# Issue order of the first loads, place of one block's statistics, and time of the last loads of x in a fused layernorm, state-space and gated-MLP kernel

## The chip, the cores and the metric

The kernel runs on one core of one Trainium2 chip. The metric is the device time in microseconds (us) of one execution. Three runs of the kernel before the change gave a median of 200.94 us (200.86 to 201.03).

## What is computed

The input x is one sequence of 2048 tokens with 512 features. The reference, cut to what matters:

```python
xn = _layernorm(x, axis=-1)
# A: a diagonal complex state-space model over the tokens
Lam_bar = exp(dt * Lam);  B_bar = ((Lam_bar - 1) / Lam)[:, None] * Bmat
Bu = einsum("bld,pd->blp", xn, B_bar)
h[t] = Lam_bar * h[t-1] + Bu[:, t]
A = 2 * einsum("blp,dp->bld", hseq, Cmat).real + xn * Dskip
# B: a gated MLP with 1792 hidden features
B = (silu(xn @ w1) * (xn @ w3)) @ w2
return x + A + B
```

The output is bfloat16, and so are x and all the weights.

## The kernel before the change, in words

**Tiling.** The 2048 tokens are four blocks (0 to 3) of 512 tokens; a block is four chunks of 128 tokens, one token on each partition. A chunk of x is 128 KB. All of x has its home in one tile, `x_all`, of which `x_blk[b]` is block b. Weights w1 and w3 are loaded by columns; a tile of 128 hidden features is called f here (f = 0 to 13).

**A block's way.** Layernorm: mean and variance of each chunk (`ln_stats`, L219 and L220, VectorE), the reciprocal root, the normalized chunk `xn` (`ln_apply`, L224), and its transpose `xnT` (TensorE and ScalarE in block 0, L243 and L244; a transposing DMA on SP's queue in the other blocks, L247). Then `glu(b)`: for each f four matmuls with w1 and four with w3 into PSUM tiles `gu_ps` (L587), copied out by ScalarE (L596, L597) and multiplied on VectorE (L604, "gate"). In the midst of it `bu(b)` makes the state inputs (L454, copied out into `u` at L456). VectorE turns `u` by tables of cosines and sines (L484, L488, L493), scans it (L505) and turns it back (L513, L519); POOL adds the two halves by accumulating DMAs (L527). Last comes `y_fast` (L1054): seven matrix products for each pair of chunks, with sums of the operands made on VectorE (L1000, L1005, L1096) and by POOL's accumulating DMAs (L1007, L1093).

**The start.** Block 0 can't wait for whole weights. L164 to L170 issue, ahead of everything: each of chunks 0 and 1 of x as two halves, the left half on SP's queue and the right half on ScalarE's; chunk 3 on ScalarE's queue and chunk 2 on SP's; then four weight loads of 256 KB on SP's queue: w1 columns 0 to 255, w3 columns 0 to 255 (for f = 0 and 1), w1 and w3 columns 256 to 511 (f = 2 and 3). TensorE runs warm-up matmuls on a tile of ones (L196), transposes chunk 0 and 1, and does `quarter(cl, fs)` (L619): 128 tokens of one chunk by the first three f. Its order is chunk 0 and then 1 with f = 0, 1; the transpose of the parameter rows (L315); transposes of chunk 2; chunk 0 with f = 2; transposes of chunk 3; chunk 1 with f = 2; then chunks 2 and 3. `bulk_loads` (L172 to L180) issues the rest of w1 and w3, x of block 1 and the state weights on SP's queue, held back by a small ScalarE instruction (L173) that reads the first reciprocal root. SP's queue is in order: a DMA that waits holds back all behind it.

**The filler.** VectorE's work for later stages stands in a queue of tasks, `bg`, each with an estimated cost; `bg.fill` and `bg.flush` take tasks from its head while the program text is built, so that the order on each engine is fixed beforehand. At the head stand (L1169 to L1174): the angles of the second half of the tables (`table_angles(2, 2)`, L376 to L380), the four chunk statistics of block 1 (`ln1a`) and the reciprocal root on POOL (`finish_stats`, L254, L255), the four `ln_apply` with their transposing DMAs (`ln1b`), and then `late_loads` (L182 to L186), which issues on SP's queue w2, the skip row, the four chunks of x of block 2, and x of block 3 in one piece. Behind these come the tasks of `ssm_tasks(0)`, block 0's state pipeline.

**Later readers that the prediction speaks of.** The x of block 2 is first read by ScalarE at L274 (sums for the layernorm of block 2). `res_list` has POOL add x of a block into `xn` by an accumulating DMA (L937). The row sums of the first pair of chunks, `row_sums(0)` (L1000), are written over the x of blocks 0 and 1, so they wait until these accumulating DMAs have read it.

Of the kernel before, what the change touches and what calls it, by code (L numbers as in the profile page):

```python
# [17 lines left out]
P = 128  # L18
# [45 lines left out]
def kernel(  # L64
# [17 lines left out]
    nc = tc.nc  # L82
    _, S, D = A_x.shape
# [25 lines left out]
    xv = A_x[0].rearrange("(c p) d -> p c d", p=P)  # L109
# [40 lines left out]
    x_all = xpool.tile([P, NBLK, CPB, D], BF16, name="x_blk")  # L150
    x_blk = [x_all[:, i] for i in range(NBLK)]
# [3 lines left out]
    def load_w(f0, f1, eng1=nc.sync, eng3=nc.sync):  # L155
        eng1.dma_start(out=w1_sb[:, :, f0:f1], in_=w1v[:, :, f0:f1])
        eng3.dma_start(out=w3_sb[:, :, f0:f1], in_=w3v[:, :, f0:f1])

    def load_x(b, parts=1):
        n = CPB // parts  # L160
        for i in range(0, CPB, n):
            nc.sync.dma_start(out=x_blk[b][:, i:i + n, :], in_=xv[:, b * CPB + i:b * CPB + i + n, :])

    for c in range(2):  # L164
        for eng, dsl in ((nc.sync, slice(0, D // 2)), (nc.scalar, slice(D // 2, D))):
            eng.dma_start(out=x_blk[0][:, c, dsl], in_=xv[:, c, dsl])  # L166
    nc.scalar.dma_start(out=x_blk[0][:, 3, :], in_=xv[:, 3, :])
    nc.sync.dma_start(out=x_blk[0][:, 2, :], in_=xv[:, 2, :])
    load_w(0, 2 * P)
    load_w(2 * P, 4 * P)  # L170

    def bulk_loads():  # L172
# [9 lines left out]
    def late_loads():  # L182
        nc.sync.dma_start(out=w2_sb, in_=B_w2.rearrange("(t p) d -> p t d", p=P))
        nc.sync.dma_start(out=dskip_row, in_=A_Dskip.partition_broadcast(P))
        load_x(2, 4)
        load_x(3)  # L186

# [23 lines left out]
    bg = Filler(LEAD)  # L211
# [37 lines left out]
    def ln_tasks_vector(b):  # L249
        csl = slice(b * CPB, (b + 1) * CPB)  # L250

        def finish_stats():
            vpe = lnp.tile([P, CPB], FP32, name="vpe")
            nc.gpsimd.tensor_scalar(out=vpe, in0=mv_all[:, csl, 1], scalar1=LN_EPS, scalar2=None, op0=ALU.add)  # L254
            nc.gpsimd.tensor_tensor(out=rstd_all[:, csl], in0=vpe, in1=mhalf, op=ALU.pow)  # L255

        def apply(cl):
            if cl == 0:
                ln_alloc(b)
            ln_apply(b, cl)  # L260
            ln_transpose(b, cl)

        first = [(0.85, lambda cl=cl: ln_stats(b, cl)) for cl in range(CPB)] + [(0.0, finish_stats)]
        second = [(0.4, lambda cl=cl: apply(cl)) for cl in range(CPB)]
        return first, second
# [74 lines left out]
    def sin_step(until=None):  # L340
        while sins and (until is None or until not in sins_done):
            key, fn = sins.popleft()
            fn()
            sins_done.add(key)
            if until is None:
                break
# [23 lines left out]
    def table_angles(pt, n=1):  # L370
        if pt + n > 3:
            sin_step((pt + n - 4, 0))
        slots = scratch[:, 0:2 * NPT * 2 * TBLK].bitcast(FP32).rearrange("p (h i t) -> p h i t", h=2, t=TBLK)
        ang, rnd = slots[:, 0, pt:pt + n, :], slots[:, 1, pt:pt + n, :]
        for i in range(n):
            nc.vector.tensor_scalar(out=ang[:, i, :], in0=iota_f, scalar1=turn[:, pt + i:pt + i + 1], scalar2=None,  # L376
                                    op0=ALU.mult)
        nc.vector.tensor_scalar(out=rnd, in0=ang, scalar1=MAGIC, scalar2=None, op0=ALU.add)
        nc.vector.scalar_tensor_tensor(out=ang, in0=rnd, scalar=MAGIC, in1=ang, op0=ALU.subtract, op1=ALU.subtract)
        nc.vector.tensor_scalar(out=rnd.bitcast(DT.int32), in0=ang.bitcast(DT.int32), scalar1=0x7FFFFFFF, scalar2=None,  # L380
                                op0=ALU.bitwise_and)
        for k in range(pt, pt + n):
            for i, (src, bias, scale) in enumerate(((rnd, halfpi, -TWO_PI), (ang, 0.0, -TWO_PI))):
                sins.append(((k, i), lambda k=k, i=i, src=src[:, k - pt, :], bias=bias, scale=scale: nc.scalar.activation(
                    out=tabe[:, k, i, :], in_=src, func=ACT.Sin, bias=bias, scale=scale)))
# [76 lines left out]
    def ssm_tasks(b, posts_last=False, between=(), middle=(), late=()):  # L462
# [76 lines left out]
        def add(*fns):  # L539
            for fn in fns:  # L540
                bg.add(0.0 if fn in transfers else 1.2 if fn in scans0 or fn in scans1 else 1.16, fn,
                       ("scan", b) if fn in scans0 else ("post", b) if fn in post0 else ("ssm", b))

        if b == 0:
            add(*pre0, *scans0, *post0, *pre1, *scans1, *post1)
            return
        add(*pre0)
        for t in middle:
# [32 lines left out]
    def glu(b):  # L581
# [76 lines left out]
        for f in range(f0, NFT):  # L658
            if f == AHEAD[b]:
                if b == 0:  # L660
                    ssm_tasks(0)
                if b == 2:
                    sin_step(("squares", 3, CPB - 1))
                    bg.flush(("bu", 0))
                    steps.extend(bu_fast(b, 0))
                    second = lambda: bu_fast(b, 1)
                else:
                    bu(b)
# [497 lines left out]

    ln_alloc(0)
    ln1a, ln1b = ln_tasks_vector(1)
    bg.add(3.6, lambda: table_angles(2, 2))  # L1169
    for t in ln1a:  # L1170
        bg.add(*t)
    for t in ln1b:
        bg.add(*t, ("ln", 1))
    bg.add(0.0, late_loads, ("ln", 1))  # L1174
    bg.add(0.2, params_w)
    gate = glu(0)
# [33 lines left out]
    def keep_ends(b):  # L1210
# [3 lines left out]
        nc.vector.tensor_copy(out=ends, in_=act(b)[:, CPB - 1].rearrange("p (h k) t -> p h k t", h=2)[:, :, NFH:NK, P - 1])  # L1214

    ssm_tasks(1, between=[(0.2, lambda: keep_ends(0))])
    gate = glu(1)
    gate()
# [6 lines left out]
    for cl, o in held:  # L1225
        nc.sync.dma_start(out=ov[:, cl, :], in_=o)
    bg.add(*difference(1))
    ssm_tasks(2, between=res_list(3), late=[(0.2, lambda: keep_ends(1)), *row_sums(2, *pairs[2]), *column_sums(3)])
    bg.first(bu_sums(2))
    gate = glu(2)  # L1230
# [52 lines left out]
```

## Time and profile before

| what | value |
|---|---|
| median of three runs | 200.94 us |
| span of the profiled execution (first to last instruction) | 199.5 us |
| around the span (median less span) | 1.4 us |
| busy: PE, DVE, ACT, POOL | 195.6, 181.8, 135.0, 51.5 us |
| share of PE in the chain that ended last | 95% |
| TensorE clock granted in the mean | 0.999 |

The page gives one time for the profiled execution, its span; the runs' times are longer by what lies ahead of the first and behind the last instruction. PE is TensorE, PEld its weight loads, DVE is VectorE, ACT ScalarE, POOL GpSimd, SPq the queue that SyncE issues DMAs on. A timeline row gives the start, the duration, the engine and line, the operation with output and inputs, the number of instructions merged into the row, and in brackets the engine's idle time ahead of it with what ended it. A row of windows gives the busy time of each engine in a stretch with the number of instructions, the granted clock, the busy share of the 16 DMA engines (over 1 where packets overlap) and the rate.

### The profile page before, as it was taken

How to read it: one execution, taken by the hardware profiler on the slowest of the kernel's cores; microseconds unless marked ns; L12 is line 12 of the kernel's file. 1: busy time of each engine (PE TensorE's matmuls, PEld its weight loads, DVE VectorE, ACT ScalarE, POOL GpSimd, SP SyncE). 2: the span in 40 equal slices, each digit the busy share in tenths (PEclk: the TensorE clock that was granted, in tenths of full speed). 3: DMA queues.
4: the chain of work that ended last, by engine and by line, in shares of the span. 5: the costliest groups of instructions: out<-in, count | busy, mean ns of one | idle time of the engine just before them, and what ended most of it. 6: DMA issues, size and time to landing. Idle time of an engine off the chain costs nothing.

```text
span 199.5 us, 3700 instructions
## 1 busy us (share of the span) xinstructions
PE 195.6 (98%) x1401; PEld 130.7 (65%) x1401; DVE 181.8 (91%) x254; ACT 135.0 (68%) x281; POOL 51.5 (26%) x75
## 2 busy tenths in 40 slices
PE   8999999999999999999999999999999999999994
PEld 2774444444444488866555468888566678888893
DVE  3689699999999999989999997999999999999972
ACT  4699897699999996968998684362588783111220
POOL 7180289700411134041202305040021303310000
PEclk9999999999999999999999999999999999999999
DMA  4999996991497054730997455838137732941111
GB/s 138 326 277 200 302 186 124 343 273 23 69 181 141 0 105 82 135 105 0 156 148 119 89 92 98 172 83 132 53 59 129 149 56 52 174 92 36 53 44 40
DMA packets 32258, 25.12 MB, mean 126 GB/s; under 512 B 16240, under 2 KB 29936, under 8 KB 32240
## 3 DMA queue, kind: packets, MB, share of 16 engines
q0 software_dynamic: 6128, 11.38, 33.5%
q1 hardware_dynamic: 25536, 13.21, 26.8%
q10 hardware_dynamic: 576, 0.30, 0.5%
q8 instruction: 11, 0.18, 0.4%
q14 instruction: 7, 0.06, 0.1%
HBM read 7.74 MB, written 2.10 MB: 49 GB/s over the span
## 4 chain that ended last, share of the span: by engine, by line
PE 95%; DMA 2%; SPq 1%; issue 0%; DVE 0%
PE gu_ps L587 34%; PE gu_ps L1054 17%; PE y_ps L1054 10%; PE gu_ps L848 7%; PE bu_ps L1054 7%; PE bu_ps L454 3%; PE y_ps L454 3%; PE y_ps L869 3%; PE y_ps L780 3%; DMA w_sb<-in_B_w_dram 2%; PE gu_ps L619 2%; PE gu_ps L780 2%; PE bu_ps L869 1%; PE bu_ps L780 1%; PE bu_ps L619 1%; SPq L166 0%
## 5 line engine op out<-in xcount | busy, mean ns | idle before, releaser
L587 PE MATMUL gu_ps<-xnT,w_sb 128*128 128x512 bf16 x312 | 69.6, 379 | 0.0
L587 PEld LDWEIGHTS <-w_sb 128*128 128x128 bf16 x312 | 30.5, 98 | 34.2
L1054 PEld LDWEIGHTS <-act 128*128 128x128 f16 x462 | 43.5, 98 | 5.4
L596 ACT ACTIVATE g<-gu_ps 128x512 bf16<-128x512 f32 x41 | 24.8, 606 | 6.0 <-PE gu_ps L587 3.6
L597 ACT ACTIVATE u<-gu_ps 128x512 bf16<-128x512 f32 x41 | 24.8, 606 | 4.5 <-PE gu_ps L587 3.7
L505 DVE TENSOR_TENSOR_SCAN u<-rho,ends,u 128x512 bf16<-128x512 f32 x16 | 20.0, 1270 | 0.0
L527 POOL DMA_DIRECT2D act<-p x7 | 9.2, 1320 | 34.0 <-DVE act L519 22.1
L1054 PE MATMUL gu_ps<-w_sb,act 128*128 128x256 bf16 (+3 forms) x126 | 16.0, 267 | 0.0
L848 PE MATMUL gu_ps<-xnT,w_sb 128*128 128x512 bf16 x64 | 15.9, 379 | 0.0
L604 DVE TENSOR_TENSOR act<-g,u 128x1024 f16<-128x1024 bf16 x21 | 14.2, 679 | 0.4 <-ACT u L597 0.4
L860 ACT ACTIVATE g<-gu_ps 128x512 bf16<-128x512 f32 x14 | 8.4, 599 | 5.4 <-PE gu_ps L848 5.0
L454 PEld LDWEIGHTS <-bt 128*128 128x128 bf16 x64 | 6.3, 98 | 7.5
L1077 ACT ACTIVATE x_blk<-gu_ps 128x256 f32<-128x256 f32 (+1 forms) x9 | 3.3, 368 | 10.6 <-PE gu_ps L1054 10.6
L1054 PE MATMUL bu_ps<-w_sb,act 128*128 128x256 bf16 (+3 forms) x84 | 10.4, 264 | 0.0
L1054 PE MATMUL gu_ps<-ct,act 128*128 128x256 f16 (+1 forms) x72 | 10.4, 267 | 0.0
L848 PEld LDWEIGHTS <-w_sb 128*128 128x128 bf16 x64 | 6.3, 98 | 4.8
L505 DVE TENSOR_TENSOR_SCAN u<-rho,u 128x512 bf16<-128x512 f32 x8 | 9.2, 1206 | 0.0
L1054 PEld LDWEIGHTS <-x_blk 128*128 128x128 f16 x88 | 8.6, 98 | 1.0
L1054 PEld LDWEIGHTS <-tw 128*128 128x128 f16 x88 | 8.6, 98 | 1.0
L513 DVE TENSOR_TENSOR p<-u,tabe 128x2048 f16<-128x2048 bf16 (+1 forms) x8 | 8.7, 1085 | 0.1
L519 DVE TENSOR_TENSOR act<-u,tabe 128x2048 f16<-128x2048 bf16 (+1 forms) x8 | 8.7, 1083 | 0.0
L488 DVE TENSOR_TENSOR u<-u,tabe 128x2048 bf16<-128x2048 bf16 x7 | 8.5, 1219 | 0.1
(203 smaller groups left out, 392.5 us busy)
## 6 DMA issues: line engine op xcount, KB each, us to landing
act<-p POOLq DMA_DIRECT2D x6, 512.0 KB, 6.1
xn<-x_blk POOLq DMA_DIRECT2D x4, 512.0 KB, 5.5
out_dram<-xn SPq DMA_DIRECT2D x15, 128.0 KB, 1.7
w_sb<-in_B_w_dram SPq DMA_DIRECT2D x1, 1792.0 KB, 8.2
act<-act POOLq DMA_DIRECT2D x5, 352.0 KB, 4.6
w_sb<-in_B_w_dram SPq DMA_DIRECT2D x2, 768.0 KB, 6.4
u<-p POOLq DMA_DIRECT2D x3, 512.0 KB, 5.1
w_sb<-in_B_w_dram SPq DMA_DIRECT2D x4, 256.0 KB, 4.9
```

The lines of the kernel that those rows point to most:

```text
L454: nc.tensor.matmul(out=ps, lhsT=bt[:, ri, dt, pt * P:(pt + 1) * P], rhs=xnT_blk[b][:, dt, :], start=(dt == 0), stop=(dt == NDT - 1))
L505: nc.vector.tensor_tensor_scan(out=v, data0=rho[:, pt:pt + 1].to_broadcast([P, TBLK]), data1=v, initial=init, op0=ALU.mult, op1=ALU.add)
L513: nc.vector.tensor_tensor(out=by_state(st["p16"][:, csl]), in0=by_chunk(st["g"][:, :, ::-1, tsl]), in1=by_chunk(tabe[:, psl, 2:0:-1, tsl]) ...
L519: nc.vector.tensor_tensor(out=by_state(act_state(b, hf)[:, csl]), in0=by_chunk(st["g"][:, :, :, tsl]), in1=by_chunk(tabe[:, psl, 0:1, tsl] ...
L527: gp.dma_start(out=a, in_=p16, accum_op=ALU.add)
L587: nc.tensor.matmul(out=ps[:, tsl], lhsT=w[:, dt, f * P:(f + 1) * P], rhs=xnT[:, dt, tsl], start=(dt == 0), stop=(dt == NDT - 1))
L596: nc.scalar.activation(out=g16[:, f % 2, :], in_=g_ps, func=ACT.Silu)
L597: nc.scalar.activation(out=u16[:, f % 2, :], in_=u_ps, func=ACT.Copy)
L604: nc.vector.tensor_tensor(out=act_gates(b, f - 1), in0=split(g16), in1=split(u16), op=ALU.mult)
L780: nc.tensor.matmul(out=out[:, h * TH:(h + 1) * TH], lhsT=left[:, h, k, :], rhs=right[:, k, :], start=(start and h == 0 and k == 0), stop=( ...
L848: nc.tensor.matmul(out=ps, lhsT=w[:, dt, f * P:(f + 1) * P], rhs=xnT[:, dt, :], start=(dt == 0), stop=(dt == NDT - 1))
L1054: nc.tensor.matmul(out=out, lhsT=left[:, k, :], rhs=right[k][:, cols], start=(start and k == 0), stop=(k == NK - 1), skip_group_check=True)
```

## The change

Chunks 0 and 1 of x are each loaded whole, chunk 0 on SP's queue and chunk 1 on ScalarE's. Right behind them go the first weights, w1 on SP's queue and w3 on ScalarE's, and only then chunks 2 and 3. In the filler, the statistics of block 1 (with the reciprocal root on POOL) move ahead of the angles of the second half of the tables. The loads of x of blocks 2 and 3 leave `late_loads`: a new task behind block 0's state pipeline has POOL write one element of a row of each of the two blocks, and the loads, which must not overtake that write, are issued on SP's queue behind it.

```diff
-    for c in range(2):
-        for eng, dsl in ((nc.sync, slice(0, D // 2)), (nc.scalar, slice(D // 2, D))):
-            eng.dma_start(out=x_blk[0][:, c, dsl], in_=xv[:, c, dsl])
-    nc.scalar.dma_start(out=x_blk[0][:, 3, :], in_=xv[:, 3, :])
-    nc.sync.dma_start(out=x_blk[0][:, 2, :], in_=xv[:, 2, :])
-    load_w(0, 2 * P)
+    def load_chunk(c, eng):
+        eng.dma_start(out=x_blk[0][:, c, :], in_=xv[:, c, :])
+
+    load_chunk(0, nc.sync)
+    load_chunk(1, nc.scalar)
+    load_w(0, 2 * P, nc.sync, nc.scalar)
+    load_chunk(3, nc.scalar)
+    load_chunk(2, nc.sync)
     load_w(2 * P, 4 * P)
...
         nc.sync.dma_start(out=dskip_row, in_=A_Dskip.partition_broadcast(P))
+
+    def last_x_loads():
+        nc.gpsimd.memset(x_all[:, 2:4, 0, 0:1], 0.0)
         load_x(2, 4)
         load_x(3)
...
             add(*pre0, *scans0, *post0, *pre1, *scans1, *post1)
+            bg.add(0.0, last_x_loads)
             return
...
     ln1a, ln1b = ln_tasks_vector(1)
-    bg.add(3.6, lambda: table_angles(2, 2))
     for t in ln1a:
         bg.add(*t)
+    bg.add(3.6, lambda: table_angles(2, 2))
     for t in ln1b:
         bg.add(*t, ("ln", 1))
```

## The prediction

> **What bounds the kernel now.** I read the page first: its busy times, and part 4, the chain of work that ended last.
>
> ```profile
> span 199.5 us, 3700 instructions
> PE 195.6 (98%) x1401; PEld 130.7 (65%) x1401; DVE 181.8 (91%) x254; ACT 135.0 (68%) x281; POOL 51.5 (26%) x75
> ...
> PE 95%; DMA 2%; SPq 1%; issue 0%; DVE 0%
> ```
>
> TensorE is busy for 98% of the span and makes up 95% of the chain. The chain in order of time says where the rest lies. Columns: start, length, what.
>
> ```profile
> 2.58 4.53 DMA w_sb<-in_B_w_dram
> 7.11 0.05 issue
> 7.16 1.51 PE gu_ps L619 x24
> ```
>
> From 7.16 to 196.81 each piece of the chain is PE. So a change can win only ahead of 9 us or so, where TensorE waits for first data, and it can lose wherever it makes TensorE wait later. The list of weight loads of TensorE (PEld) at the start shows the waits.
>
> ```profile
> 6.27 0.45 PEld L619 LDWEIGHTS <-w_sb 128*128 128x128 bf16 x8 [0.18 <-DMA w_sb<-in_B_w_dram]
> 7.15 1.34 PEld L619 LDWEIGHTS <-w_sb 128*128 128x128 bf16 x24 [0.44 <-DMA w_sb<-in_B_w_dram]
> 8.60 0.09 PEld L315 LDWEIGHTS <-par_rows 12*128 12x128 bf16 x1
> 8.71 0.23 PEld L243 LDWEIGHTS <-xn 128*128 128x128 bf16 x4
> 8.89 0.62 PEld L619 LDWEIGHTS <-w_sb 128*128 128x128 bf16 x8
> ```
>
> Three waits for weights: 0.18 us for w1 (f = 0, 1), 0.44 us for w3, and a hidden one: eight loads take 0.45 us in the row at 6.27 and 0.62 us at 8.89, so 0.17 us for the second w3 piece. Together 0.79 us. That is all this end of the kernel has to give.
>
> **Part 1, the first loads.** No byte is added. SP's first weight load is its second DMA instead of its fourth: issued at about 1.15 instead of 2.11 us. The w3 load is the second on ScalarE's queue, at about 1.15 instead of 2.58. ScalarE still issues three DMAs ahead of its table load. Is there room for weights to come sooner? The windows say yes (columns: length, busy of PE, PEld, DVE, ACT, POOL, granted clock, DMA share, GB/s):
>
> ```profile
> 3.00:4.50 1.50, 1.50 (x5) 0.44 (x3) 1.39 (x3) 0.79 (x3) 1.43 (x4) 1.00 0.55 174
> 4.50:9.00 4.50, 4.05 (x52) 2.85 (x51) 3.46 (x11) 3.12 (x12) 0.12 (x3) 1.00 1.12 316
> ```
>
> Between 3.0 and 4.5 us the DMA engines are half idle; from there to 9 us they are full. 1.5 x 0.45 = 0.68 us can be made up. The first two weight pieces, 512 KB, take 1.7 us at 316 GB/s, and chunks 0 and 1 are in before the second statistics at 3.90: weights by 5.6 us or earlier, ahead of TensorE's need at 6.1. These two waits go. The second w3 piece stands behind the same 1.25 MB as before; it can come at most 0.68 us sooner, and TensorE wants it 0.18 + 0.44 + 0.17 = 0.79 us sooner. So about 0.7 of 0.79 at best.
>
> Two things are taken off. First, chunk 0 now shares the engines with chunk 1. VectorE's first statistics start at 3.08 on its landing. If a whole chunk lands like a half did (2.1 us after issue), that is 0.2 us earlier; if only when both chunks were in, up to 0.8 us later (3.90). I take 0.1 us later, near to the half's row, since the bytes of both chunks were already nearly all in by then. Second, chunks 2 and 3 now stand behind 512 KB of weights. Their bytes come after 1.7 + 0.8 us of transfer, so at about 5.9 to 6.4 us, and VectorE wanted chunk 2 at 5.72. Its normalized chunk was ready at 7.75 for a transpose at 8.71, which moves to 8.1; chunk 3's at 8.43 for 9.47, which moves to 8.7: a slack of 0.3 us each. I take 0.15 us of loss from it, with ends at 0 and 0.4.
>
> Net gain of part 1: 0.79 - 0.1 - 0.15 = 0.54 us; ends 0.1 and 0.8.
>
> A rule bears on this. The Trainium skill, "DMA: Bandwidth & Descriptors", section "Issuing engines are not separate DMA queues", says that spreading DMAs over the issuing engines saves only the sequencer's issue time, as all run on the same 16 DMA engines. By it alone the gain would be the issue time, 0.4 to 0.9 us of earlier start, and nothing in bandwidth; the half-idle window agrees that the start was short of issued work.
>
> **Part 2, block 1's statistics ahead of the angles.** The same VectorE instructions in another order. What it takes away is VectorE's wait for POOL's root:
>
> ```profile
> 23.54 0.41 DVE L224 TENSOR_SCALAR xn<-x_blk,mv_all,rstd_all 128x512 bf16<-128x512 bf16 x1 [1.47 <-POOL rstd_all L255]
> ...
> 25.17 0.60 ACT L456 ACTIVATE u<-y_ps 128x512 bf16<-128x512 f32 x1 [0.27 <-PE y_ps L454]
> ...
> 26.02 1.23 DVE L484 TENSOR_TENSOR p<-u,tabe 128x2048 bf16<-128x2048 bf16 x1
> ```
>
> In the new order the root is made while VectorE does the angles (3.6 us), so the 1.47 us go. But L484 at 26.02 reads `u`, whose last quarter ScalarE ends at 25.17 + 0.60 = 25.77. VectorE can come forward by 0.2 us only; the other 1.2 us turn into a wait for ScalarE. VectorE is not on the chain here. Later angles reach their readers, the sine steps from 25.66 on, in time (ready by 22.4). The gate moved behind the statistics frees its buffers some 3 us later, still ahead of the next copy that needs them. Value: 0; ends 0 and 0, as TensorE waits for no VectorE result before 70 us.
>
> **Part 3, x of blocks 2 and 3 later.** In the program of the changed kernel POOL's small write stands behind the second accumulate of block 0 (L527, issued 50.95 for 1.28 us) and ahead of the first L937. So five loads, 1 MB, are issued on SP from about 52.2 to 54.7 instead of 33.47 to 36.5. Behind them on SP stand only the transposes of block 2, first needed at 77. The first reader, L274, comes at 61.92; the slowest such load of before took 8.1 us, which gives 60.3: no wait. POOL pays 0.1 us.
>
> The price is contention.
>
> ```profile
> 46.50:52.50 6.00, 6.00 (x29) 2.74 (x28) 5.97 (x8) 5.90 (x11) 1.55 (x2) 1.00 0.00 0
> 52.50:59.00 6.50, 6.50 (x32) 2.94 (x30) 6.43 (x8) 6.37 (x12) 1.50 (x2) 1.00 1.00 164
> ```
>
> The loads would have been free up to 52.5 us, but they come when POOL's accumulates (L527, L937) already fill the DMA engines. 1 MB at 343 GB/s (the rate from 9 to 12.5 us) is 3.1 us of all engines. L937, issued at 52.08, landed 6.9 us later, at 59.0; VectorE's L1000 must wait for it, since it overwrites what L937 reads, and started at 59.50. From there VectorE runs without a gap to the row that TensorE needs:
>
> ```profile
> 59.50 0.88 DVE L1000 TENSOR_TENSOR x_blk<-act 128x1408 f16<-128x1408 f16 x1
> ...
> 73.77 0.88 DVE L1096 TENSOR_TENSOR act<-act,x_blk 128x1408 f16<-128x1408 f16 x1
> ```
>
> L1096 ends at 74.65, and the product that reads it starts at 75.86: 1.1 us of slack. So a delay C of L937 stops TensorE for C - 0.5 - 0.2 - 1.1 = C - 1.8 us (0.5 is the margin at L1000, 0.2 the lead from part 2), if that is positive. C lies between 0 (the loads queue behind the accumulates) and 3.1 us (all of them pass first). Nearest rows: an accumulate issued at 37.56, after 2.9 MB of loads, took 9.1 us to land instead of 5.5; and transposes issued at 96.85, after two accumulates, landed 7.0 us later instead of 3.7 in the median. So what is issued later also waits. The loads go out within a microsecond of L937: I share evenly, C = 1.5, a stall of 0; ends 0 and 1.3 us.
>
> The same page, section "Queues, rings and completion order", says that each DMA engine goes round-robin between its queues, a packet at a time. By it C would be an estimated 2 to 2.7 us and the stall up to 0.9.
>
> What the earlier stretch wins (from 33.5 to 44 us the DMA share is 1.04) stands on nobody's path: the accumulate at 37.56 landed at 46.6, its reader started at 47.69.
>
> **Sum.** 199.5 - 0.54 + 0 + 0 = 199.0 us of span; with 1.44 us around it (200.94 less 199.5) 200.4 us. A measurement of this kernel can tell about 0.2%, 0.4 us.
>
> **Rivals.**
> - *Forecast, 0.55:* gain at the start, no new stall: 200.15 to 200.6.
> - *The start gains little, 0.15:* chunks 2 and 3 come late, or the second w3 piece stays where it was (same bytes ahead of it). For: its slack is 0.3 us, and the DMA engines are full from 4.5 us. Against: the half-idle 1.5 us. Gain 0.1 to 0.3: 200.7.
> - *Half a stall, 0.13:* C about 2.4, so 0.6 us of the gain goes back: 200.9 to 201.1.
> - *Slower, 0.17:* the 1 MB passes ahead of L937 whole. It decides from C = 2.3, where the stall passes 0.5 us and eats the gain; at C = 3.1 it is 1.3 us, so 200.94 - 0.54 + 1.3 = 201.7. For: full DMA engines from 52.5 to 59. Against: the accumulate of 50.95 is ahead of all loads.
>
> Faster by over 0.2% (below 200.54): nine tenths of the forecast, 0.50. Within: 0.05 + 0.15 + 0.10 = 0.30. Slower: 0.17 + 0.03 = 0.20. The range goes from 200.1 to 201.3; the top of the last case and a sliver below are left out, less than 2 in 10.
>
> **What would show it.** Right: the weight loads at L619 start by 6.2 with no wait for w1 and w3, the main run of matmuls (13.04 in the chain) starts near 12.5, VectorE waits for `u` instead of the root near 25, PE has no gap near 75. Wrong: a wait of VectorE for chunk 2 that reaches the transposes at 8 to 9 us; L1000 beginning after 61 us and a PE gap ahead of the product that reads L1096; ScalarE waiting at L274 for x.

## The result: 1.0% slower, and the profile after

The changed kernel took 203.04 us in the median (202.96 to 203.27, 5 runs) beside 200.94 us for the kernel before (200.79 to 201.86, 5 runs): a ratio of 1.0103, with a 95% interval of 1.0087 to 1.0118. The forecast was 200.4 us, inside 200.1 to 201.3; the time lies above all of it. The span of the profiled execution grew from 199.5 to 201.3 us.

In the changed file the lines behind the start are 5 or 6 higher: L219 is now L224, L224 is L229, L587 is L593, L619 is L625, L937 is L943, L1000 is L1006, L1054 is L1060, L1096 is L1102.

The page of the changed kernel, with busy times and the chain that ended last:

```profile
span 201.3 us, 3699 instructions
PE 195.5 (97%) x1401; PEld 130.7 (65%) x1401; DVE 181.6 (90%) x254; ACT 135.1 (67%) x281; POOL 47.0 (23%) x76
...
PE 70%; DVE 18%; DMA 6%; issue 4%; ACT 0%; POOL 0%; POOLq 0%; DVEq 0%
```

TensorE does the same work, and the chain, which was PE for 95%, now runs through VectorE and a DMA for a quarter of the span. Its pieces in order of time name them (start, length, what):

```profile
57.31 8.60 DMA xn<-x_blk
65.91 0.03 issue
65.94 0.05 DVEq L1006
65.99 0.04 issue
66.04 0.89 DVE x_blk L1006
...
76.62 0.81 DVE act L1102
77.42 0.05 issue
77.47 1.38 PE bu_ps L1060 x11
```

The DMA is the **second** accumulate into `xn` (x of block 1). VectorE waits for it at the second row sum, and from there on everything on VectorE is late, up to the row that TensorE needs. The timelines of the two engines put sizes to it:

```profile
60.21 0.89 DVE L1006 TENSOR_TENSOR x_blk<-act 128x1408 f16<-128x1408 f16 x1 [0.99 <-DMA xn<-x_blk]
66.04 0.89 DVE L1006 TENSOR_TENSOR x_blk<-x_blk,act 128x1408 f16<-128x1408 f16 x1 [1.95 <-DMA xn<-x_blk]
...
76.53 0.88 DVE L1102 TENSOR_TENSOR act<-act,x_blk 128x1408 f16<-128x1408 f16 x1
```

```profile
77.47 0.94 PE L1060 MATMUL bu_ps<-w_sb,act 128*128 128x256 bf16 x7 [1.60 <-DVE act L1102]
```

L1096 started at 73.77 before and L1102 starts at 76.53 now: 2.76 us late. TensorE had 1.1 us of slack and stops for 1.60 us, its only stop behind 10 us. The windows say what the DMA engines did meanwhile (columns as in the prediction's windows):

```profile
52.00:59.50 7.50, 7.50 (x36) 3.43 (x35) 7.16 (x9) 7.37 (x14) 1.68 (x2) 1.00 1.04 174
59.50:66.00 6.50, 6.50 (x31) 2.94 (x30) 3.88 (x6) 6.37 (x16) 0.86 (x1) 1.00 1.05 256
```

A row of the kernel before:

```profile
59.00:64.00 5.00, 5.00 (x25) 2.25 (x23) 5.00 (x8) 4.90 (x11) 0.86 (x1) 1.00 0.95 177
```

From 52 to 66 us the DMA engines of the changed kernel are full without a break; VectorE is busy for 3.88 of the last 6.5 us. Before, the accumulates alone kept the DMA engines nearly full from 59 to 64 us (0.95), and VectorE worked without a gap. By the trace the five loads of x are issued from 52.02 to 57.0 and land from 56.7 to 63.6. Three of the four chunk loads land at 60.4 to 61.0 and the 512 KB of block 3 at 63.60, all ahead of the second accumulate, which lands at 65.91 instead of 62.75.

At the start, the weight loads of TensorE and the first statistics of VectorE:

```profile
6.64 1.83 PEld L625 LDWEIGHTS <-w_sb 128*128 128x128 bf16 x32
```

```profile
3.69 0.70 DVE L224 BATCH_NORM_STATS2 stats<-x_blk 128x6 f32<-128x512 bf16 x1 [3.69 <-DMA x_blk<-in_A_x_dram]
```

The waits for weights are gone: 32 loads in one run. But this run begins at 6.64, while the first weights were in use from 6.27 before, because VectorE's statistics start 0.61 us later (3.69 instead of 3.08).

### The profile page after: what moved, and what is told of

Read it like the earlier page. It is cut to its first block, busy times and chain, and to the rows that moved or that the text cites. A ratio compares the mean times of both kernels' runs of the same rounds, so it can differ in the third digit from the quotient of the medians.

```text
span 201.3 us, 3699 instructions
## 1 busy us (share of the span) xinstructions
PE 195.5 (97%) x1401; PEld 130.7 (65%) x1401; DVE 181.6 (90%) x254; ACT 135.1 (67%) x281; POOL 47.0 (23%) x76
## 4 chain that ended last, share of the span: by engine, by line
PE 70%; DVE 18%; DMA 6%; issue 4%; ACT 0%; POOL 0%; POOLq 0%; DVEq 0%
PE gu_ps L1060 17%; PE gu_ps L593 16%; PE y_ps L1060 8%; PE gu_ps L854 7%; PE bu_ps L1060 5%; DMA xn<-x_blk 4%; DVE u L510 4%; PE y_ps L875 3%; PE y_ps L786 3%; DVE act L610 3%; DVE u L493 2%; DVE p L489 2%; PE gu_ps L625 2%; PE gu_ps L786 2%; DMA x_blk<-in_A_x_dram 1%
## 5 line engine op out<-in xcount | busy, mean ns | idle before, releaser
L593 PE MATMUL gu_ps<-xnT,w_sb 128*128 128x512 bf16 x312 | 69.6, 379 | 0.0
L593 PEld LDWEIGHTS <-w_sb 128*128 128x128 bf16 x312 | 30.5, 98 | 34.2
L1060 PEld LDWEIGHTS <-act 128*128 128x128 f16 x462 | 43.4, 98 | 7.3 <-DVE act L1102 1.9
L1060 PE MATMUL gu_ps<-w_sb,act 128*128 128x256 bf16 (+3 forms) x126 | 16.0, 267 | 0.0
L1060 PE MATMUL bu_ps<-w_sb,act 128*128 128x256 bf16 (+3 forms) x84 | 10.4, 264 | 1.6 <-DVE act L1102 1.6
L1060 PE MATMUL gu_ps<-ct,act 128*128 128x256 f16 (+1 forms) x72 | 10.4, 267 | 0.0
L1060 PEld LDWEIGHTS <-x_blk 128*128 128x128 f16 x88 | 8.6, 98 | 1.0
L1060 PEld LDWEIGHTS <-tw 128*128 128x128 f16 x88 | 8.6, 98 | 1.0
L224 DVE BATCH_NORM_STATS2 stats<-x_blk 128x6 f32<-128x512 bf16 x8 | 5.4, 672 | 3.7 <-DMA x_blk<-in_A_x_dram 3.7
```

The lines of the kernel that those rows point to most:

```text
L593: nc.tensor.matmul(out=ps[:, tsl], lhsT=w[:, dt, f * P:(f + 1) * P], rhs=xnT[:, dt, tsl], start=(dt == 0), stop=(dt == NDT - 1))
L1060: nc.tensor.matmul(out=out, lhsT=left[:, k, :], rhs=right[k][:, cols], start=(start and k == 0), stop=(k == NK - 1), skip_group_check=True)
```

## The experiments

The theory after the result: the late loads of x occupy the DMA engines while the accumulates into `xn` are on their way, the second accumulate pays for most of the bytes, and VectorE's wait for it stops TensorE. Rivals: POOL's extra write or the longer SP queue costs the time; one of the other two parts does. Each kernel computes all of the output. Each ratio is to the kernel before on the same chip. That took 201.05 us in the median beside the four kernels under "Which part"; 201.35 beside the write without the loads, half the bytes late, the same bytes at another time, and halves first; and 200.99 beside the other three.

### Which part

**Part 1 alone:** the kernel before with the new first loads in place of the old ones.

```diff
...
+    load_chunk(0, nc.sync)
+    load_chunk(1, nc.scalar)
+    load_w(0, 2 * P, nc.sync, nc.scalar)
+    load_chunk(3, nc.scalar)
+    load_chunk(2, nc.sync)
...
```

> Part 1 alone on the kernel before. Theory: chunk 0 lands 0.6 us later, which takes back 0.6 of the 0.8 us that the three weight waits were worth: 200.6 to 200.9 us. Rival (the later landing of chunk 0 was chance of one profile): 200.2 to 200.5 us with the first statistics near 3.1.

Measured: 201.18 us, ratio 1.0008 (0.9995 to 1.0020). No gain that can be seen; the time lies above what the theory and the rival gave.

**Part 2 alone:** the kernel before with the angles behind the statistics.

```diff
-    bg.add(3.6, lambda: table_angles(2, 2))
     for t in ln1a:
         bg.add(*t)
+    bg.add(3.6, lambda: table_angles(2, 2))
```

> Part 2 alone on the kernel before. Theory: VectorE's wait of 1.5 us for the root turns into one for the state inputs u; TensorE doesn't see it: 200.8 to 201.1 us. Rival (VectorE's order costs or gains on the path): off by more than 0.4 us either way.

Measured: 201.09 us, ratio 1.0011 (0.9997 to 1.0025). Nothing.

**Part 3 alone:** the kernel before with the late loads of x.

```diff
+    def last_x_loads():
+        nc.gpsimd.memset(x_all[:, 2:4, 0, 0:1], 0.0)
         load_x(2, 4)
         load_x(3)
...
+            bg.add(0.0, last_x_loads)
```

> The kernel before with part 3 alone: x of blocks 2 and 3 loaded behind POOL's small write. Theory (the loads crowd out POOL's two accumulates into xn, and VectorE waits for both at its row sums): slower by 1.5 to 2.0 us against before, 202.5 to 203.0 us, a PE gap of about 1.6 us at the product that reads VectorE's fourth sum, VectorE waiting at both row sums. Rival (the loss comes from the other order of VectorE's work or from the first loads): 200.9 us, no gap.

Measured: 204.45 us (202.81 to 205.49, 4 runs), ratio 1.0143 (1.0106 to 1.0180): the loss is here, and it is larger than I expected. Its timeline of TensorE:

```profile
78.37 0.94 PE L1058 MATMUL bu_ps<-w_sb,act 128*128 128x256 bf16 x7 [1.99 <-DVE act L1100]
```

VectorE waited 1.06 and 2.07 us for the two accumulates, and TensorE 1.99 us for the row that is L1096 in the kernel before. What came on top is told under the hardware below.

**Parts 1 and 2 without part 3:** the changed kernel with x of blocks 2 and 3 back in `late_loads`.

> The changed kernel with the loads of x put back where they were: parts 1 and 2. Theory: the start gains 0.16 us as in the changed kernel's profile, nothing is lost later: 200.6 to 200.9 us, no PE gap after 10 us. Rival (parts 1 and 2 cost something as well): 201.5 to 203 us.

Measured: 201.15 us, ratio 1.0009 (0.9996 to 1.0023); no wait at the row sums and no stop of TensorE behind 10 us. The gain of 0.16 us that was expected from the start doesn't show. So part 3 carries the whole loss.

### What in part 3

**The write without the loads:** the changed kernel with the loads early again and POOL's write on a tile that nothing uses, at the same place.

```diff
+    idle = const.tile([P, 2], BF16, name="idle")
     def last_x_loads():
-        nc.gpsimd.memset(x_all[:, 2:4, 0, 0:1], 0.0)
-        load_x(2, 4)
-        load_x(3)
+        nc.gpsimd.memset(idle, 0.0)
```

> The changed kernel with all loads of x early as before, and POOL's small write at its place in the changed kernel, on a tile that nothing else uses. Theory (the loads cost the time, not POOL's extra instruction ahead of the accumulates): 200.9 to 201.3 us, no wait of VectorE for an accumulate over 0.2 us. Rival (POOL's write, 0.62 us ahead of the first accumulate, is a large part of the delay): 201.8 us or more.

Measured: 201.18 us, ratio 0.9995 (0.9986 to 1.0004), no wait of VectorE at the row sums. The write costs nothing: POOL issues the accumulate 1.13 us after the one ahead of it, with the write between them as without.

**Half the bytes late:** the changed kernel with x of block 3 early, and only the 512 KB of block 2 late.

```diff
         nc.sync.dma_start(out=dskip_row, in_=A_Dskip.partition_broadcast(P))
+        load_x(3)
     def last_x_loads():
-        nc.gpsimd.memset(x_all[:, 2:4, 0, 0:1], 0.0)
+        nc.gpsimd.memset(x_all[:, 2:3, 0, 0:1], 0.0)
         load_x(2, 4)
-        load_x(3)
```

> The changed kernel, but only x of block 2 (four loads, 512 KB) is loaded late; x of block 3 (512 KB) goes out early as before. Theory (the delay of the accumulates grows with the bytes that pass ahead of them): the second accumulate lands some 1.5 us later than before instead of 3.2, VectorE's two waits are together 1 to 1.5 us instead of 2.9, TensorE's gap near 77 us 0 to 0.3 us; time 200.9 to 201.5 us. Rival (the delay does not depend on the amount; an accumulate is held up by any load beside it): waits of nearly 3 us and 202.5 to 203 us.

Measured: 201.30 us, ratio 0.9998 (0.9988 to 1.0008). The view of tile `xn` lists the two accumulates' time from issue to landing. The kernel before, the half and the changed kernel in turn:

```profile
DMA to landing us min/median/max: 5.1/6.0/6.9
```

```profile
  DVE x_blk L1006: 1.2, 2
...
DMA to landing us min/median/max: 6.9/7.5/8.1
```

```profile
  DVE x_blk L1006: 2.9, 2
...
DMA to landing us min/median/max: 8.5/8.5/8.6
```

The first line of the last two is who waited and how long: VectorE 1.2 and 2.9 us in all. The trace tells the two accumulates apart. The second took 5.1, 6.9 and 8.6 us: 1.8 us more for 512 KB and 3.5 for 1 MB, in proportion to the bytes. The first took 6.9, 8.1 and 8.5 us: the second half of the bytes added only 0.3 us to it, so it pays for the first few loads. With half the bytes the waits stay within TensorE's slack, TensorE doesn't stop and the time is that of before. So the loss sets in with a threshold: VectorE's waits come to 1.2 us here and cost nothing, to 2.9 us in the changed kernel and cost 1.60.

**The same bytes at another time:** the changed kernel, but VectorE does the small write, ahead of the second half of block 0's state work.

```diff
-        nc.gpsimd.memset(x_all[:, 2:4, 0, 0:1], 0.0)
+        nc.vector.memset(x_all[:, 2:4, 0, 0:1], 0.0)
...
-            add(*pre0, *scans0, *post0, *pre1, *scans1, *post1)
-            bg.add(0.0, last_x_loads)
+            add(*pre0, *scans0, *post0, *pre1)
+            bg.add(0.1, last_x_loads)
+            add(*scans1, *post1)
```

> The changed kernel, but VectorE instead of POOL does the small write that holds the loads of x of blocks 2 and 3 back, and does it before the second half of block 0's state work instead of behind it: the five loads still go out late, but at about 42 to 46 us, in the stretch of 46.5 to 52 us in which the DMA engines of both kernels stand idle. Theory (the loads cost time only because they share the DMA engines with the accumulates into xn, issued at 52 and 57 us): the accumulates land at about 59.0 and 62.8 us as in the kernel before, VectorE has no wait for them ahead of the row sums (or under 0.2 us), TensorE no gap near 77 us; time 200.8 to 201.2 us. Rival (late loads cost time whatever they meet, by the write, the wait on the SP queue or the transposes behind them): 202 us or more.

Measured: 201.15 us, ratio 0.9995 (0.9986 to 1.0004). The view of the loads on SP's queue, of the changed kernel and of this one (columns: shortest, median and longest issue in ns, first and last start):

```profile
L162 SPq DMA_DIRECT2D x_blk<-in_A_x_dram x5: 341/1228/1330, 52.0 to 55.7; - x5
...
DMA to landing us min/median/max: 4.7/7.6/8.0
```

```profile
L162 SPq DMA_DIRECT2D x_blk<-in_A_x_dram x5: 340/430/434, 42.4 to 44.2; - x5
...
DMA to landing us min/median/max: 2.0/2.5/4.3
```

Ten microseconds earlier, with hardly anything beside them, the same loads land in a third of the time, and the accumulates take 7.1 and 5.3 us (6.9 and 5.1 before). Loading x late costs nothing as such; meeting the accumulates does.

**The same bytes behind the accumulates:** the changed kernel with the task behind `res_tasks(1)`, so that the loads go out behind the second accumulate (issued at 57.07; loads from 58.07).

```diff
-            bg.add(0.0, last_x_loads)
...
     res_tasks(1)
+    bg.add(0.0, last_x_loads)
```

> The changed kernel with POOL's small write, and so the loads of x of blocks 2 and 3, behind the second accumulate into xn (issued at about 57.5 us) instead of ahead of the first. Theory A (an accumulate is delayed by the bytes that were issued ahead of it): both accumulates land as in the kernel before (near 59.0 and 62.8 us), VectorE doesn't wait for them over 0.3 us; the price moves to ScalarE, whose first sum of block 2's x (61.8 us in the changed kernel) waits 1 to 3 us for its chunk; time 201 to 202.5 us. Theory B (queues share the engines whatever was first): the second accumulate lands 1 us or more later than before, VectorE waits about 1 us for it; time 201.2 to 203 us.

Measured: 201.22 us, ratio 1.0006 (0.9991 to 1.0020). The accumulates take 7.1 and 5.3 us: theory A. The price moves to ScalarE, as it said, at the lower end of what was expected:

```profile
62.79 0.63 ACT L279 ACTIVATE xn<-x_blk 128x512 bf16<-128x512 bf16 x1 [1.17 <-DMA x_blk<-in_A_x_dram]
```

ScalarE waits 1.17 us for block 2's first chunk, and TensorE waits for none of it. So here the order of issue settles who pays: what was issued 1 us ahead of the loads was hardly held up by them (5.3 us instead of 5.1).

### What the start has to give

**Halves first, then the weights:** the kernel before with the first weights on two queues and chunks 2 and 3 behind them, the halves kept.

```diff
+    load_w(0, 2 * P, nc.sync, nc.scalar)
     nc.scalar.dma_start(out=x_blk[0][:, 3, :], in_=xv[:, 3, :])
     nc.sync.dma_start(out=x_blk[0][:, 2, :], in_=xv[:, 2, :])
-    load_w(0, 2 * P)
```

> The kernel before with one edit at the head: chunks 0 and 1 in halves on two queues as before, then the first weights on the two queues, then chunks 3 and 2. Theory (the whole-chunk loads gave away 0.6 us at the first statistics, the weights' earlier start wins 0.8 us): first statistics start at 3.1 to 3.2 us, no wait of TensorE for weights, main run of matmuls 0.5 to 0.8 us earlier than before; time 200.2 to 200.6 us. Rival (the bytes of chunks 0 and 1 share the DMA engines with the weights whichever way they are cut, or something else in the head is late instead): first statistics 3.5 us or later, or a new wait; 200.9 to 201.2 us.

Measured: 201.38 us, ratio 1.0004 (0.9993 to 1.0016). The first statistics start at 2.90 and there is no wait for weights, but VectorE waits 0.91 us for chunk 2 and so does TensorE, in its weight loads:

```profile
8.64 0.23 PEld L243 LDWEIGHTS <-xn 128*128 128x128 bf16 x4 [0.69 <-DVE xn L224]
```

The rival held: something else in the head is late instead.

**Weights between the chunks:** halves; then chunk 2 and w3 on ScalarE's queue, w1 and chunk 3 on SP's.

```diff
-    nc.scalar.dma_start(out=x_blk[0][:, 3, :], in_=xv[:, 3, :])
-    nc.sync.dma_start(out=x_blk[0][:, 2, :], in_=xv[:, 2, :])
-    load_w(0, 2 * P)
+    nc.scalar.dma_start(out=x_blk[0][:, 2, :], in_=xv[:, 2, :])
+    load_w(0, 2 * P, nc.sync, nc.scalar)
+    nc.sync.dma_start(out=x_blk[0][:, 3, :], in_=xv[:, 3, :])
```

> The kernel before with one edit at the head: halves of chunks 0 and 1 as before; then chunk 2 and the first w3 on ScalarE's queue, the first w1 and chunk 3 on SP's. Theory (the first stage needs 1 MB of x and weights, which the DMA engines have in by about 7 us in any order; an order only chooses who waits, and weights between the chunks make nobody wait long): first statistics near 3.0 us, waits of TensorE for weights and for normalized chunks together under 0.4 us ahead of 9.5 us instead of 0.79, the run of 56 weight loads starting at 9.2 to 9.4 instead of 9.70; time 200.7 to 201.2 beside about 201.1 for the kernel before, hardly to be told apart. Rival (the order alone set the waits, and a good one wins the whole 0.8 us): run of 56 at 8.9, time 200.2 to 200.5 us.

Measured: 201.49 us, ratio 1.0017 (1.0003 to 1.0030). Neither theory's numbers held: in its profile w3 landed at 7.88, TensorE waited 0.33 us for w1 and 1.15 us for w3, and the run of 56 weight loads began at 10.34 instead of 9.70. This profile is of the longest of its runs (202.07 us), and with the old order w3 landed as late as 7.86 in a profile. The order may cost something here, 0.17% with an interval that just leaves out zero; that is not more than a hint.

**Both late chunks on ScalarE's queue,** so that the weights are SP's third and fourth DMAs.

```diff
-    nc.scalar.dma_start(out=x_blk[0][:, 3, :], in_=xv[:, 3, :])
-    nc.sync.dma_start(out=x_blk[0][:, 2, :], in_=xv[:, 2, :])
+    nc.scalar.dma_start(out=x_blk[0][:, 2, :], in_=xv[:, 2, :])
+    nc.scalar.dma_start(out=x_blk[0][:, 3, :], in_=xv[:, 3, :])
     load_w(0, 2 * P)
```

> The kernel before with one edit at the head: chunk 2 is issued on ScalarE's queue ahead of chunk 3 instead of on SP's, so that the first w1 and w3 are SP's third and fourth DMAs (at about 1.65 and 2.1 us instead of 2.11 and 2.58). Theory (bytes, not issue times, set the head): w1 and w3 land at most 0.4 us sooner and chunks 2 and 3 no sooner; TensorE's waits for weights 0.4 to 0.8 us; time 200.8 to 201.3 us, no change. Rival (issue time sets it): both weights 0.5 us sooner, waits 0.2 us or less, time 200.4 to 200.7 us.

Measured: 201.31 us, ratio 1.0007 (0.9995 to 1.0020); w1 landed at 6.11 and w3 at 7.36 (6.22 and 7.11 before), although issued 0.5 us sooner, and TensorE waited 0.81 us for w3. The earlier issue won nothing.

Of all the kernels none is faster than the kernel before by more than its interval.

## Why the prediction was wrong

**The step that failed** is in part 3: "L937, issued at 52.08, landed 6.9 us later", and from it one delay C and a stall of C - 1.8. There are two accumulates, and the second, issued at 57.67 for the second row sum at 63.29, was left out. Its reader lies in the rows that the prediction passed over between 59.50 and 73.77, and it had the same margin of 0.5 us, landing at 62.75. It is also issued 5.6 us later, with all five loads already ahead of it, so it pays for their bytes: 3.2 us later by the clock, near the upper end of 3.1 us that the prediction held for the first. The first landed 1.2 us later, inside the range; by the same sum it stops nothing, as was forecast for it, since the row sum that it holds up started 0.71 us late (60.21 instead of 59.50) and the slack is 1.1. The row of the kernel before that the second accumulate holds up:

```profile
63.29 0.88 DVE L1000 TENSOR_TENSOR x_blk<-x_blk,act 128x1408 f16<-128x1408 f16 x1
```

With the right accumulate the prediction's sum comes out. The delay of 3.2 us less the margin of 0.54 makes VectorE 2.6 us late; measured at L1102 were 2.76 (the row sum starts 0.13 us behind the landing, at 66.04). Less 1.1 us of slack that is 1.5 to 1.66 us; measured were 1.60. The 0.2 us of lead that the prediction took off is in this already: from issue to landing the second accumulate lost 3.5 us, and 0.36 us of it came back because it was issued that much earlier (57.31 instead of 57.67).

**C = 1.5 by sharing evenly** was right in size for the accumulate that it was made for: from issue to landing the first one lost 1.55 us (8.47 instead of 6.92). That was partly luck, since with half of the bytes late it still lost 1.2 us, where half of the share would be some 0.8. The Trainium skill, "DMA: Bandwidth & Descriptors", section "Queues, rings and completion order", has each DMA engine go round-robin between its queues by packet, from which the prediction estimated 2 to 2.7 us for it: more than was measured. The runs side with neither rule: the accumulate issued with the loads (its issue ran from 51.72 to 52.83 us, theirs began at 52.02) lost 1.55 us from issue to landing, the one issued behind all of them 3.5, and the one issued 1 us ahead of them 0.2. An even exchange between two queues would not make the last so small; order of issue explains more.

**The rival "slower"** had the mechanism: 1 MB passes ahead of an accumulate whole. It had chosen the first one and so a point (C from 2.3 us) that the first one, with 1.55, does not reach; its time was 201.7 us at most and its chance 0.17.

**Part 1: two terms.** The 0.79 us of waits for weights went as forecast, and chunks 2 and 3 cost nothing instead of 0.15. "I take 0.1 us later" for chunk 0 was mis-sized: in this profile it is 0.61, inside the ends that the prediction gave. Over the profiles of all kernels, the first statistics start at 2.90 to 3.10 us where chunks 0 and 1 come in halves (six profiles) and at 3.33 to 3.69 where they come whole (seven). In the changed kernel chunk 0 lands at 3.66 us and chunk 1 at 3.89, so a whole chunk lands when nearly both are in. That sharing the engines with the other chunk is the reason is argued and not tried by itself: the weights, too, are issued sooner behind whole chunks (1.17 us; behind halves 1.64 at the earliest).

The main run of TensorE began at 12.88 us instead of 13.04: a gain of 0.16 and not 0.54. These are two single executions, and the start differs between executions of one order: the run of 56 weight loads begins at 9.70, 10.05 and 10.31 us in three profiles of the old order and at 9.28 to 9.69 in seven of the new. In the medians of all runs part 1 alone wins nothing. So the rival "the start gains little" came nearer here, though not for its reasons. Three other orders of the same bytes won none of what "this end of the kernel has to give" either: with halves first a wait for weights became a wait for x, and in the other two TensorE waited 1.15 and 0.81 us for w3.

**Part 2** went as forecast: VectorE's 1.47 us for POOL's root became 1.46 us for ScalarE (1.2 was expected), and the run of it alone shows no change.

```profile
25.63 1.23 DVE L489 TENSOR_TENSOR p<-u,tabe 128x2048 bf16<-128x2048 bf16 x1 [1.46 <-ACT u L461]
```

**POOL's 0.1 us** for the write is zero, and ScalarE didn't wait at the first sum of block 2's x: both as forecast or better.

**The time around the span** was taken as 1.44 us, a median of runs less the span of one execution. In the later runs, each with its own span, the kernel before shows 1.8 (201.08 with 199.3), and the changed kernel 1.74 (203.04 with 201.3). So the profiled execution of before was itself some 0.3 us above the median run, and the forecast was too low by that much.

**The sum.** The forecast span was 199.0 and 201.3 was measured. Of these 2.3 us, 1.60 are TensorE's stop; 0.18 its first group of products behind it (1.38 us instead of 1.20); 0.38 the missing gain at the start; the last 0.12 lie behind TensorE's end, where 2.86 us follow the last product instead of 2.74 (so in all seven kernels with the new first loads; why was not looked at). With 0.3 around the span this makes the 2.6 us between 200.4 and 203.04.

The chain bears this out. From the start of the main run to the end of the last product it takes 183.75 us before (13.04 to 196.79) and 185.53 in the changed kernel (12.88 to 198.41): 1.78 more, the stop and the slower group behind it. In the profiles of the ten other kernels without such a stop this stretch is as long as before within 0.04 us. What else differs between their spans lies ahead of the main run and behind the last product.

## What to carry to other kernels

A moved load has to be set against every DMA that is in flight or issued after it, each with its reader and that reader's margin, and not only against the one nearest in time; the one behind all of the moved bytes paid for all of them here (3.5 us for 1 MB). Look for a stretch in which the DMA engines stand idle, and put the transfer there (here 42 to 48 us instead of 52 to 57), or issue it behind the DMA that must not wait. When several transfers together have to be in before an engine can run, another order may only choose who waits, as the four orders of the first loads did here.

## What the runs showed of the hardware

**A stop of TensorE was followed by a slower clock.** In the profile of part 3 alone the stop of 1.99 us is followed by half the granted clock (windows; the third number from the end):

```profile
78.00:80.00 2.00, 1.63 (x14) 1.43 (x15) 1.97 (x5) 1.59 (x3) 1.31 (x2) 0.92 0.18 35
80.00:83.00 3.00, 3.00 (x16) 2.13 (x15) 2.70 (x5) 1.60 (x3) 0.00 (x0) 0.50 1.01 178
83.00:86.00 3.00, 3.00 (x29) 2.65 (x28) 2.21 (x2) 2.15 (x7) 0.00 (x0) 0.99 1.09 133
```

Half the clock from about 79.7 to 83.0 us costs some 1.7 us more. Its span of 203.7 us is 4.2 above the 199.5 of before: 1.99 for the stop, 0.17 for the first group of products behind it, 1.7 for the clock, 0.35 for weights that came later in this execution. Two of its four runs show a mean clock of 0.992, and they are its longest (204.89 and 205.49 us); the other two took 202.81 and 204.01. The changed kernel's stop of 1.60 us left the clock at 1.00 in all its runs. That the stop lowers the clock is argued from this order and not tried by itself; why the run of 204.01 us was that long stays open. The Trainium skill, "TensorE: Matmul & The Clock Gate", section "What's actually happening", has half the clock follow on an idle window of about 3.4 us, and the full clock on a busy one of that length. The depth (0.50) and the length of the slow stretch (about 3.3 us) agree with it; a full idle window does not show, as here a stop of 1.99 us came ahead of it.

**Issuing took longer beside the accumulates.** SP took 0.34 to 0.43 us to issue each of the five loads at 42 to 44 us, when hardly anything else was under way, 0.34 to 1.33 us beside the accumulates in the changed kernel, and up to 2.10 us behind the second accumulate. Full engines alone did not do that: in the kernel before it took 0.43 to 0.73 us for the same loads at 33.5 to 36.5 us, with a DMA share of 1.04 from 33.5 to 44.

**The start differs from execution to execution.** With the old order of the first loads w3 landed at 7.11, 7.60 and 7.86 us in three profiles, so its wait is not a fixed 0.44 us.
